# Linear attention and feed-forward on one core: w_phi loaded behind ScalarE's table load, and another order of steps behind the first key tile

## Chip, core, metric

The kernel runs on one core of a Trainium2 chip. The metric is the device time of one execution in microseconds (us). Before the change three runs took 228.24, 227.59 and 227.71 us, so the median is 227.71 us.

## What is computed

A block of a network over S = 2048 tokens of width D = 640 with H = 32 heads of 20 columns. `A` is linear attention with a learned feature map, `B` is a feed-forward layer of width 1728:

```python
qkv   = layernorm(x) @ wqkv                      # q, k, v: 32 heads x 20
pq,pk = q @ w_phi[h], k @ w_phi[h]               # per head, 20 x 20
phi   = concat(softmax(p), softmax(-p))          # 40 features of a head
kv, z = phi_k.T @ v, sum(phi_k)                  # over all 2048 tokens
o     = (phi_q @ kv) / (phi_q . z + 1e-6)
h     = x + o @ wo
out   = h + silu(layernorm(h) @ w1) @ w2
```

All tensors are bfloat16.

## The kernel before

The 2048 tokens are 16 tiles of 128 rows. The whole program is one list of named steps, ORDER; a step emits its instructions, and each engine and each DMA queue executes its own in the order of that list. Engines run beside each other and wait only for data and for buffers. So ORDER is six queues at once: TensorE, VectorE, ScalarE, GpSimd, SyncE with its DMAs, and ScalarE's own DMA queue, which only w_phi uses.

**Start.** Weights come in with X. `phi_a` and `phi_b` (VectorE, L305 and L308) make block-diagonal copies of w_phi's columns from the tile WPH, which is loaded by L183. `wk`, `fk` on TensorE transpose the key weights and fold phi into them (Wfk); `fq` (L437) does the same for queries, from the tile WTq, which the six steps `wq` (L425) load through a transposing DMA from DRAM.

**Keys, tile t.** `st` moments (VectorE), `rs` and `xn` normalise the row, `xt` transposes it into XnT: by TensorE for tiles 0 to 3, by a transposing DMA on SyncE's queue (L552) from tile 4 on. `K` and `V` (TensorE, L571, ten matmuls each) project, `ex` (ScalarE, L626) exponentials, `su` sums (VectorE, L630), `rk` inverse (ScalarE, L638 and L639), `sc` scale (VectorE, L643), `ve` copies the values (ScalarE), `kv` accumulates (TensorE, L662, eleven matmuls). `load0` to `load10` are the loads of wo, w1 and w2 (L563), which nothing needs before the later stages; they lie in SyncE's queue among the `xt`.

**Queries and attention.** `Q` (L609), `qe`, `qs`, `ql`, `qi`, `qr`, then `qt`, a transposing DMA into EqT. `bd` (VectorE) makes KVB from the accumulated kv. `D` (L817) applies it, `E` (VectorE, L826 and L827) divides, `ot` transposes O by a DMA (L839), `G` (L849, two steps of five matmuls for a tile) multiplies by wo, `ga` adds the residual (L856), `lm`, `ls`, `lr`, `hn`, `ht` are the second layernorm and its transpose.

**Feed-forward.** `u` (L931) and `s` (Silu) by units of two or four tiles. The product with w2 goes by pairs of tiles as seven products of half blocks in place of eight (`p1` to `p7`, L1036), with sums of weights (`T`, L1001) and of rows (`S`, L1018) ahead of them on VectorE, and `r`, `w` behind. `p7` needs S3 and T3; `p1` and `p2` need no sums. `out` stores.

**PSUM.** The key stage rotates three pairs of banks (`ps_pair`); a K, V, Q or fq step takes the pair whose last user lies three steps back, and waits until ScalarE or VectorE has read it. Later eight banks go round a ring.

Of the kernel before, what the change touches and what calls it, by code (L numbers as in the profile page):

```python
# [27 lines left out]
rk5 V8 ve8 V9 load4 rk7 sc5 st12 fq5 ve9 st14 rk6 xn11 rs12 K8 fq5e xt10 ref9 rs13 xn12 ex8 sc6 kv5 sc7
K9 su8 ref10 load1 V10 ex9 ve10 load5 kv6 eqr0 rs14 su9 Q0 K10 rk8 xn13 kv7 Q1 xt12 qe0 ref11 xt11 sc8
rk9 ref12 st15 sc9 xt13 xn14 kv8 rs15 K12 kv9 ex10 V12 su10 qe1 ex12 load0 K11 qs1 ve12 K13 xt14 rk10  # L30
su12 ex11 load10 qs0 ref13 V11 sc10 kv10 xn15 ex13 xt15 K14 su11 ql1 ve11 eqr1 rk12 V13 su13 qi1 ref15
# [10 lines left out]
D9 u2.0 u2.4 s2.12 u2.11 qs11 s2.0 ot8 s2.3 ls6 G81 G80 u2.7 qr10 qr11 E9 s2.11 u2.6 lr6 s2.6 qs14 s2.4
qt10 ga8 qs12 u2.5 qr12 lm8 u2.8 D10 out0 ot9 E10 qt11 s2.5 u2.10 hn6 ls8 G90 s2.7 u2.1 s2.8 s2.10 u2.9
out1 G91 qr14 u2.2 qs13 qr13 qt12 ga9 ot10 D11 s2.1 lt2 E11 ht6 s2.9 s2.2 S3.2 lm9 qt13 S1.2 ot11 lr8
hn8 ls9 p2.2 ht8 p1.2 lr7 D12 r1.2 S2.2 qt14 G101 G100 p7.2 p6.2 E12 r7.2 p4.2 lr9 hn7 ht7 G110 S4.2 hn9
ga10 S3.4 r2.2 w11.2 w21.2 G111 ot12 ga11 p7.4 p5.2 w22.2 lm10 r3.2 ht9 ls10 D13 lm11 ls11 p3.2 S1.4
p1.4 G121 S2.4 lr11 u6.1 r7.4 G120 r1.4 p6.4 w12.2 E13 p4.4 s6.1 ot13 ga12 D14 r2.4 w21.4 out3 E14 lm12
p5.4 ls12 lr12 u6.L w22.4 G131 r3.4 ot14 hn11 qs15 u6.3 G130 s6.L u6.2 qr15 u6.0 u6.9 ht11 s6.2 lr10
ga13 s6.0 p2.4 lm13 s6.9 w11.4 out5 hn12 u6.7 s6.3 hn10 G140 G141 u6.11 out2 s6.7 qt15 ht12 ls13 D15
S4.4 lr13 ht10 u6.12 u6.4 u6.10 s6.11 E15 ga14 hn13 s6.4 ht13 p3.4 w12.4 u6.5 u10.L ot15 s6.10 u6.8 s6.5  # L50
u6.6 s10.L lm14 s6.12 G151 s6.6 G150 lt6 S3.6 s6.8 S1.6 u10.2 ls14 p1.6 S2.6 r1.6 ga15 lm15 p7.6 r7.6
p6.6 u10.3 s10.2 p2.6 p4.6 S4.6 u10.6 s10.3 r2.6 p5.6 u10.8 u10.11 u10.9 lr14 s10.8 w21.6 S3.8 w22.6
r3.6 w11.6 p3.6 p7.8 hn14 p1.8 S1.8 s10.6 S2.8 ht14 u10.7 r1.8 p2.8 ls15 s10.9 p6.8 s10.11 s10.7 w11.8
lt10 w12.6 r7.8 u10.0 out4 u10.1 p4.8 r2.8 p5.8 lr15 u10.4 u10.10 r3.8 hn15 s10.0 w21.8 w22.8 u10.12
ht15 s10.4 s10.10 s10.12 u10.5 s10.1 u14.2 S4.8 s10.5 s14.2 S3.10 u14.12 u14.0 p2.10 out7 p7.10 S3.12
S1.10 s14.0 p3.8 p1.10 r7.10 S2.10 S4.10 out6 u14.10 p4.10 w12.8 s14.12 u14.L r1.10 u14.4 p6.10 s14.10
w11.10 p1.12 r2.10 p5.10 w21.10 u14.6 p7.12 w22.10 S1.12 s14.4 p2.12 s14.L r3.10 r7.12 r1.12 p3.10 S2.12
out8 s14.6 p4.12 w11.12 S3.14 p6.12 w12.10 out9 u14.8 s14.8 lt14 r2.12 w21.12 out11 p5.12 w22.12 p1.14
r3.12 S4.12 p7.14 S1.14 p3.12 out10 r7.14 S2.14 r1.14 p4.14 p6.14 out13 p2.14 S4.14 r2.14 w12.12 w11.14
w21.14 p5.14 p3.14 w22.14 out12 out140 r3.14 w12.14 out15 p3.14x out141 w12.14x out142  # L60
""".split()


# [1 line left out]
def kernel(  # L65
# [117 lines left out]
    nc.scalar.dma_start(WPH[:], A_w_phi.rearrange("h d f -> (h d) f").rearrange("(r p) f -> p r f", p=P))  # L183
# [15 lines left out]
    nc.scalar.preload_act_table_set("natural_log_exp_and_others")
# [935 lines left out]
```

## Time and profile before

| what | value |
|---|---|
| times of three runs, us | 228.24, 227.59, 227.71 |
| profiled execution, us | 227.59, of which the span is 225.7 |
| busy in the span | TensorE 218.2, VectorE 173.9, ScalarE 146.1, GpSimd 70.0 us |
| HBM read, written | 9.55, 2.62 MB |

A page of the profile lists busy time, the chain of work that ended last, the groups of instructions, and the DMAs. The other views are the waits (who waited for whom), the timeline (instructions in order of time, neighbours of one kind merged), and the answers for one line or one tile. `PE` is TensorE's matmul, `PEld` its weight load, `DVE` VectorE, `ACT` ScalarE, `POOL` GpSimd, `SPq` and `ACTq` the DMA queues of SyncE and ScalarE. In a timeline the columns are start, duration, engine, line, operation, output and input, count, and in brackets the idle time before it with what ended it.

### The profile page before, as it was taken

The numbers are of one execution on the slowest core, as the hardware profiler recorded it, in microseconds if no ns is written. First come the engines' busy times: TensorE is split into PE (matmuls) and PEld (weight loads), VectorE is DVE, ScalarE is ACT, GpSimd is POOL, SyncE is SP. The second block draws the span as 40 slices with busy tenths as digits, with TensorE's granted clock in tenths as the row PEclk, the third lists the DMA queues.
The fourth block names the chain that finished last, engine by engine and source line by source line (L and its number), as shares of the span: only waits on it lengthen the run. The fifth ranks groups of instructions, "written<-read, shape, count | busy, mean of one in ns | idle before, by whom it ended". The sixth has DMA issues, their size and how long they took to land.

```text
span 225.7 us, 5046 instructions
## 1 busy us (share of the span) xinstructions
PE 218.2 (97%) x1927; PEld 154.4 (68%) x1937; DVE 173.9 (77%) x305; ACT 146.1 (65%) x321; POOL 70.0 (31%) x136
## 2 busy tenths in 40 slices
...
GB/s 170 292 345 162 202 98 116 183 120 198 292 94 182 128 96 143 174 102 92 148 73 144 143 154 123 61 117 109 75 23 0 11 75 87 0 23 79 32 29 87
DMA packets 68158, 26.98 MB, mean 120 GB/s; under 512 B 61159, under 2 KB 67111, under 8 KB 68007
## 3 DMA queue, kind: packets, MB, share of 16 engines
...
q14 instruction: 8, 0.07, 0.1%
HBM read 9.55 MB, written 2.62 MB: 54 GB/s over the span
## 4 chain that ended last, share of the span: by engine, by line
PE 75%; DVE 14%; DMA 5%; issue 2%; ACT 2%; DVEq 0%; ACTq 0%
PE banks L931 25%; PE banks L1036 23%; PE banks L849 10%; PE banks L571 7%; PE banks L609 5%; DVE st L478 4%; DMA XnT<-xn 3%; PE banks L817 2%; DVE EK L643 2%; DVE Sk L630 2%; DMA OT<-O 2%; DVE Sq L737 1%; DVE xn L494 1%; PE banks L662 1%; ACT EK L626 1%
## 5 line engine op out<-in xcount | busy, mean ns | idle before, releaser
L931 PE MATMUL banks<-HnT,w_sb 128*128 128x512 bf16 (+1 forms) x315 | 59.8, 335 | 0.5
L954 ACT ACTIVATE shT<-banks 128x512 bf16<-128x512 f32 (+1 forms) x53 | 30.0, 587 | 45.2 <-PE banks L931 44.8
L931 PEld LDWEIGHTS <-w_sb 128*128 128x128 bf16 x325 | 31.2, 98 | 21.1
L571 PEld LDWEIGHTS <-XnT 128*128 128x128 bf16 x300 | 28.5, 98 | 10.9 <-DMA XnT<-xn 1.3
L494 POOL TENSOR_SCALAR xn<-X,mv,rs 128x640 bf16<-128x640 bf16 x12 | 30.8, 2565 | 1.5 <-ACT rs L485 1.3
L516 POOL TENSOR_SCALAR rs<-mv 128x1 f32<-128x1 f32 x16 | 4.7, 296 | 82.8 <-ACT xn L509 82.6
L1036 PEld LDWEIGHTS <-S 128*128 128x128 bf16 x231 | 22.1, 98 | 8.5
L1036 PE MATMUL banks<-T,S 128*128 128x320 bf16 x168 | 26.2, 299 | 0.0
L1051 DVE TENSOR_TENSOR o_t<-banks,r 128x320 bf16<-128x320 f32 (+2 forms) x33 | 15.1, 476 | 13.4 <-PE banks L1036 13.1
L849 PE MATMUL banks<-wo_sb,OT 128*128 128x320 bf16 x160 | 25.0, 299 | 0.4 <-DMA OT<-O 0.4
L1044 DVE TENSOR_TENSOR r<-banks,X 128x320 f32<-128x320 f32 x32 | 15.2, 485 | 12.9 <-PE banks L1036 12.8
L737 DVE TENSOR_REDUCE Sq<-EQ 128x66 f32<-128x1320 bf16 x16 | 24.3, 1519 | 0.0
L609 PE MATMUL banks<-Wfq,XnT 128*128 128x342 bf16 (+2 forms) x160 | 22.8, 293 | 0.0
L733 ACT ACTIVATE EQ<-banks 128x342 bf16<-128x342 f32 (+2 forms) x52 | 21.6, 527 | 1.9 <-PE banks L609 1.7
L571 PE MATMUL banks<-Wfk,XnT 128*128 128x304 bf16 x150 | 21.7, 292 | 1.0 <-DMA XnT<-xn 1.0
L571 PE MATMUL banks<-Wv,XnT 128*128 128x320 bf16 x150 | 22.5, 299 | 0.0
L630 DVE TENSOR_REDUCE Sk<-EK 128x64 f32<-128x1216 bf16 x16 | 21.9, 1402 | 0.4 <-ACT EK L626 0.4
L1036 PEld LDWEIGHTS <-shT 128*128 128x128 bf16 x168 | 16.3, 98 | 6.9
L626 ACT ACTIVATE EK<-banks 128x608 bf16<-128x608 f32 x32 | 20.3, 695 | 0.8 <-PE banks L571 0.8
L849 PEld LDWEIGHTS <-OT 128*128 128x128 bf16 x160 | 15.3, 98 | 7.4 <-DMA OT<-O 0.6
L609 PEld LDWEIGHTS <-XnT 128*128 128x128 bf16 x160 | 15.0, 97 | 5.4
L504 ACT ACTIVATE xn<-X 128x640 bf16<-128x640 bf16 x16 | 11.9, 745 | 10.0 <-DVE X L856 10.0
...
## 6 DMA issues: line engine op xcount, KB each, us to landing
...
```

The lines of the kernel that those rows point to most:

```text
L494: eng.tensor_scalar(out=xn_[t][:], in0=X[:, t, :], scalar1=mv_.pop(t)[:, 0:1], scalar2=rs_.pop(t)[:], op0=ALU.subtract, op1=ALU.mult,)
L571: nc.tensor.matmul(ps[:, g, 0:w], XnT[:, c, t * P : (t + 1) * P], W[:, c, g * w : (g + 1) * w], start=(c == 0), stop=(c == C - 1),)
L609: nc.tensor.matmul(ps[:, 0 : e - a], XnT[:, c, t * P : (t + 1) * P], Wfq[:, c, a:e], start=(c == 0), stop=(c == C - 1),)
L626: nc.scalar.activation(E5[:, :, :, b, 0:DR], p4, AF.Exp, scale=sign)
L630: nc.vector.tensor_reduce(sk[t][:], ek[t][:, 0 : H * HF].rearrange("p (q f) -> p q f", f=DH)[:, :, 0:DR], axis=AX.X, op=ALU.add)
L733: nc.scalar.activation(features(t, a, b)[:, :, :, i, 0:DR], p4, AF.Exp, scale=sign)
L737: nc.vector.tensor_reduce(sq[t][:], EQ[0][:, t, :, 0:FCH].rearrange("p c (q f) -> p c q f", f=DH), axis=AX.X, op=ALU.add)
L849: nc.tensor.matmul(ps_of["G", t][:, g, 0:HD], ot[t][:, c, :], wo_sb[:, c, g * HD : (g + 1) * HD], start=(c == 0), stop=(c == C - 1),)
L931: nc.tensor.matmul(ps[:, at : at + n], w1_sb[:, c, fc * P : fc * P + P], HnT[u][:, c, 0:n], start=(c == 0), stop=(c == C - 1),)
L954: nc.scalar.activation(rows_of(u)[:, f0 * n : f1 * n], ps_of.pop(("u", u, f0))[:, 0 : (f1 - f0) * n], AF.Silu)
L1036: nc.tensor.matmul(ps[:, lo:hi], left[:, c, :], right[:, c, lo:hi], start=(c == 0 and k in FIRST), stop=(c == KS - 1 and k in LAST), skip_ ...
L1044: nc.vector.tensor_tensor(r_[t, name][:], ps_of[bank, t][:, 0:HD], X[:, t + i, g * HD : (g + 1) * HD], op=ALU.add)
```

## The change

Two edits. The DMA that loads w_phi into WPH is emitted after the load of ScalarE's function table, where it was emitted before it; both lie on ScalarE's queue. And ORDER differs from its 105th step on, behind `xt3`: the same 899 steps with another sequence, on every engine and on SyncE's queue. No instruction is added or removed, no step changes its engine or its size.

```diff
-    nc.scalar.dma_start(WPH[:], A_w_phi.rearrange(...))
     w1_v = B_w1.rearrange("(c p) n -> p c n", p=P)
 ...
     nc.scalar.preload_act_table_set("natural_log_exp_and_others")
+    nc.scalar.dma_start(WPH[:], A_w_phi.rearrange(...))
```

The first lines of ORDER that differ, and those that hold the first attention tiles and the first products:

```diff
-wph0 K0.4 rs3 rs2 st4 K0.3 K1 V0.2 xn2 xt2 st5 ex0 rs4 ex1 V0.1 wph1 x2 V1 X8 ve1 xn3 wq3 xt3 V0.4 x3
-wq2 xn4 wq0 rs5 ve0 xn5 su0 rk0 V2 su1 st6 st7 rs6 sc0 K2 V3 xn6 rk1 ve2 xt4 ones5 rs7 K3 sc1 st11 kv0
-ex2 st8 kv1 ve3 ex3 load7 phq xt5 ones2 K4 rs8 load6 su3 ex4 rk3 xt6 su2 wq1 sc3 V4 st9 ve4 fq3 fq3e rk2
-xn7 V5 ref5 ve5 sc2 fq0 fq0e st13 rs9 K5 ref6 ex5 xn8 K6 fq2 kv2 ref7 ex6 xt7 su4 fq2e xn9 kv3 wq5 V6
-ve6 fq1 st10 fq1e K7 V7 zeros rs10 su5 xt8 rk4 sc4 fq4 xt9 ex7 ve7 rs11 kv4 fq4e ref8 ones6 xn10 su6 su7
 ...
+wph0 K0.4 rs3 rs2 st4 K0.3 K1 V0.2 xn2 xt2 st5 ex0 rs4 ex1 V0.1 wph1 x2 V1 X8 ve1 xn3 xt3 su0 st6 rk0
+xn4 V0.4 su1 x3 load10 ones5 wq0 sc0 K2 st7 rs5 st9 ve0 V2 xn5 rs6 xt4 xn6 ex2 rk1 sc1 ve2 ones2 rs9
+st12 wq3 xt5 phq V3 kv0 rs7 ve3 xt6 K3 K4 xn7 V4 ref5 kv1 ex3 ex4 st8 rs8 su2 su3 ve4 fq0 fq0e V5 fq3
+ref6 st10 rk2 xn8 ve5 wq2 K5 xn9 rk3 xt7 fq3e sc2 ex5 K6 ex6 kv2 wq1 sc3 su4 kv3 ref7 V6 su5 fq2 rk4 ve6
+K7 V7 rs12 fq2e ref8 su6 xn12 sc4 kv4 fq1 rs10 ex7 ve7 xt8 st15 rk6 ones6 xt9 fq1e zeros V8 st11 su7 fq4
+xn10 st14 ref9 ve8 rs11 wq5 sc6 rk5 fq4e xt12 xt10 rk7 V9 load7 sc5 ve9 K8 xn11 K9 sc7 fq5 kv5 fq5e kv6
 ...
-Q5 halves qt0 bd1 D0 qr2 D1 qe5 qs3 load9 Q4 qt2 E0 qe4 ql3 Q10 qe10 D2 E1 qs5 qi3 qr3 Q6 qe6 ot0 ot1
-G00 G01 ql5 qs4 E2 Q9 ql4 ga0 qi5 G11 qe9 qt3 G10 qr5 Q11 lm0 qi4 ls0 D3 qr4 ot2 lr0 qs6 ga1 Q8 qe11 lm1
+load5 qi2 halves qr2 qe7 D0 D1 qs3 ql3 E0 load6 Q4 qe4 Q10 qi3 qt2 E1 qr3 qs5 qe10 qs4 ql5 Q6 qe6 ot0 D2
+ot1 Q9 qe9 qi5 ql4 qr5 E2 G00 G01 ga0 lm0 ls0 qi4 G11 G10 qt3 Q11 qs6 qr4 D3 ga1 qe11 qt5 E3 lm1 lr0 hn0
 ...
-T2.0 lt0 u0.0 s0.6 G41 qr9 qt8 ot6 s0.12 G40 D8 s0.0 hn2 ot7 T2.1 p2.0 G61 T3.1 lr5 hn5 ga4 S1.0 p1.0
-S3.0 ls3 S2.0 p7.0 G60 lr3 lm4 E8 ht5 r1.0 ls4 G71 S4.0 lr4 w11.0 p6.0 ga6 hn3 T4.1 p3.0 r2.0 hn4 r7.0
+u0.12 ot6 s0.2 T2.2 D8 lr5 s0.8 T3.1 T3.0 lt0 ls3 S3.0 s0.10 ga4 hn5 E8 s0.12 ot7 T2.0 p7.0 S1.0 G61
+p1.0 T4.1 S2.0 p2.0 r1.0 r7.0 G60 ht2 p6.0 T4.0 T4.2 lr3 p4.0 G71 S4.0 r2.0 p3.0 lm4 p5.0 qr9 ls4 lr4
```

More of the change, by code (lines that the diff above doesn't have):

```diff
@@ L27 @@
-ve6 fq1 st10 fq1e K7 V7 zeros rs10 su5 xt8 rk4 sc4 fq4 xt9 ex7 ve7 rs11 kv4 fq4e ref8 ones6 xn10 su6 su7
[L28 to L31, printed above, removed]
@@ L32 @@
-eqp rk11 sc11 ql0 ref14 K15 qr1 rk13 load8 mask1 sc12 ex14 ve13 sc13 ex15 kv11 load2 Q2 V15 V14 qe2 su14
-qi0 su15 rk14 qr0 rk15 load3 ve14 Q3 qt1 ve15 sc14 kv12 kv13 sc15 kv14 qe3 kv15 Q7 qs2 ql2 qe7 qi2 bd0
-Q5 halves qt0 bd1 D0 qr2 D1 qe5 qs3 load9 Q4 qt2 E0 qe4 ql3 Q10 qe10 D2 E1 qs5 qi3 qr3 Q6 qe6 ot0 ot1
-G00 G01 ql5 qs4 E2 Q9 ql4 ga0 qi5 G11 qe9 qt3 G10 qr5 Q11 lm0 qi4 ls0 D3 qr4 ot2 lr0 qs6 ga1 Q8 qe11 lm1
-G20 E3 qs7 qr6 G21 qt5 Q12 hn0 ls1 ot3 ga2 lr1 qt4 qe8 Q13 qr7 D5 G31 E5 G30 hn1 ht0 ht1 ga3 qe12 qs8
@@ L37 @@
-Q14 ot5 qe13 qt6 qe14 Q15 qe15 padL0 D4 T1.0 qr8 u0.L u0.8 padL1 T1.2 E4 G50 G51 qt7 T3.0 lm2 s0.L T1.1
-ga5 s0.8 lm3 u0.10 s0.10 ls2 lm5 D6 T2.2 u0.4 u0.2 ot4 E6 D7 qs9 u0.6 u0.12 T3.2 s0.2 s0.4 E7 ls5 lr2
-T2.0 lt0 u0.0 s0.6 G41 qr9 qt8 ot6 s0.12 G40 D8 s0.0 hn2 ot7 T2.1 p2.0 G61 T3.1 lr5 hn5 ga4 S1.0 p1.0
-S3.0 ls3 S2.0 p7.0 G60 lr3 lm4 E8 ht5 r1.0 ls4 G71 S4.0 lr4 w11.0 p6.0 ga6 hn3 T4.1 p3.0 r2.0 hn4 r7.0
-T4.0 G70 p5.0 T4.2 ht2 qs10 ht3 ga7 p4.0 lm7 r3.0 ht4 qt9 w21.0 lm6 w12.0 u2.L ls7 s2.L u2.3 u2.12 w22.0
@@ L42 @@
[L42 to L60, printed above, removed]
+wph0 K0.4 rs3 rs2 st4 K0.3 K1 V0.2 xn2 xt2 st5 ex0 rs4 ex1 V0.1 wph1 x2 V1 X8 ve1 xn3 xt3 su0 st6 rk0
@@ new lines @@
+load3 kv7 ex8 ex9 st13 rs14 rs13 eqr0 su8 Q0 qe0 su9 ref10 rk8 rk9 xn13 K10 ref12 xn14 ex10 xt11 V10 sc8
+ve10 ref11 load9 Q1 kv8 V12 rs15 xn15 xt13 K12 qs0 qe1 su10 sc9 kv9 rk10 ve12 ref13 K11 load1 ex12 K13
+ex11 sc10 qs1 su12 xt14 ql0 ex13 ql1 V11 su11 su13 eqr1 rk12 rk11 load4 qi0 ve11 kv10 K14 xt15 sc11 rk13
+V13 ref14 sc12 eqp qr0 qi1 ex14 ve13 qr1 sc13 ref15 K15 load0 Q2 ex15 load2 kv11 kv12 su14 kv13 su15 V15
+qe2 qt0 rk14 qt1 rk15 V14 sc14 ve14 sc15 mask1 load8 ve15 Q3 qs2 kv14 ql2 kv15 Q5 bd0 qe3 qe5 Q7 bd1
@@ new lines @@
+load5 qi2 halves qr2 qe7 D0 D1 qs3 ql3 E0 load6 Q4 qe4 Q10 qi3 qt2 E1 qr3 qs5 qe10 qs4 ql5 Q6 qe6 ot0 D2
+ot1 Q9 qe9 qi5 ql4 qr5 E2 G00 G01 ga0 lm0 ls0 qi4 G11 G10 qt3 Q11 qs6 qr4 D3 ga1 qe11 qt5 E3 lm1 lr0 hn0
+Q8 ls1 D5 ot2 qt4 Q13 qr6 G20 qs7 lr1 G21 qe8 hn1 Q14 qe13 E5 Q15 qe14 ot3 Q12 ga2 G31 G30 ht0 qe15 qe12
+padL0 qs8 ht1 D4 u0.L ot5 T1.2 T1.0 qr7 s0.L T1.1 u0.0 lm2 padL1 qt6 ga3 E4 qt7 u0.6 qs9 G50 s0.0 qr8
+lm3 G51 T2.1 s0.6 D6 u0.4 ls2 s0.4 ga5 E6 u0.8 D7 ot4 lr2 lm5 qt8 u0.10 T3.2 u0.2 E7 G41 G40 ls5 hn2
@@ new lines @@
+u0.12 ot6 s0.2 T2.2 D8 lr5 s0.8 T3.1 T3.0 lt0 ls3 S3.0 s0.10 ga4 hn5 E8 s0.12 ot7 T2.0 p7.0 S1.0 G61
+p1.0 T4.1 S2.0 p2.0 r1.0 r7.0 G60 ht2 p6.0 T4.0 T4.2 lr3 p4.0 G71 S4.0 r2.0 p3.0 lm4 p5.0 qr9 ls4 lr4
+G70 ga6 hn3 ht5 w21.0 qs11 hn4 w22.0 ga7 ht3 ht4 u2.L lm6 u2.9 s2.L u2.1 qt9 r3.0 u2.7 ot8 w11.0 lm7
+w12.0 lt2 qr11 u2.10 s2.9 qs10 G81 qt11 s2.1 qr10 qs12 D9 u2.3 s2.3 s2.7 qt10 G80 E9 u2.5 ls6 lr6 u2.4
+s2.10 u2.2 ga8 u2.6 D10 ls7 u2.0 ot9 qr12 qt12 qs13 u2.12 s2.4 E10 lm8 D11 hn6 s2.5 ls8 ot10 u2.8 s2.0
@@ new lines @@
+qs14 E11 s2.6 s2.12 lr7 lr8 u2.11 G90 qr13 s2.2 D12 hn7 hn8 S3.2 ht6 s2.8 G91 p7.2 G101 qr14 ga9 s2.11
+S1.2 p1.2 S2.2 E12 G100 r1.2 out0 p2.2 ga10 qt13 ot11 lm9 p6.2 qt14 S4.2 D13 r2.2 r7.2 G110 G111 w11.2
+ls9 out1 S3.4 p4.2 E13 p5.2 ot12 ga11 lr9 w21.2 ht7 hn9 ht9 ht8 w22.2 ot13 D14 p7.4 r3.2 E14 lm11 p3.2
+qs15 S1.4 p1.4 S2.4 ls11 G121 r1.4 lm10 u6.L ls10 G120 u6.8 lr10 p6.4 r7.4 p4.4 ga12 S4.4 r2.4 lm12 qr15
+G131 w12.2 ot14 w21.4 G130 ga13 qt15 s6.L hn10 ls12 ht10 p5.4 lr11 s6.8 u6.11 G140 lm13 hn11 s6.11 u6.4
@@ new lines @@
+s6.4 lr12 D15 G141 u6.2 hn12 ls13 out3 r3.4 w22.4 p2.4 u6.5 s6.5 s6.2 E15 ga14 lr13 hn13 u6.1 w11.4 ht12
+u6.0 u6.3 lt6 u6.10 u6.7 out2 s6.10 s6.7 s6.3 s6.1 p3.4 w12.4 ht11 ht13 u6.6 s6.0 u10.L ot15 u6.12 u10.2
+s6.12 u10.9 s10.L G151 G150 s6.6 u6.9 S3.6 s10.2 u10.11 s6.9 S1.6 ga15 S2.6 lm15 u10.0 p7.6 s10.9 p1.6
+u10.6 lt10 lm14 S3.8 r1.6 s10.0 r7.6 s10.11 u10.7 s10.6 s10.7 u10.12 p4.6 S4.6 p6.6 p2.6 s10.12 r2.6
+p5.6 r3.6 ls15 w11.6 w21.6 u10.5 p2.8 S1.8 ls14 u10.3 w22.6 out5 lr15 u10.1 s10.5 p7.8 lr14 p1.8 S2.8
@@ new lines @@
+s10.3 hn14 u10.4 hn15 s10.1 r1.8 s10.4 ht14 w11.8 S3.10 p3.6 p6.8 ht15 r7.8 S4.8 u10.8 p4.8 out4 u14.4
+r2.8 w21.8 w12.6 s14.4 u10.10 p5.8 s10.8 w22.8 p3.8 r3.8 out6 u14.2 out9 w12.8 s14.2 s10.10 S1.10 u14.12
+p7.10 u14.10 out7 u14.L s14.12 u14.0 u14.6 p1.10 out8 S3.12 s14.0 s14.L r7.10 lt14 u14.8 S2.10 r1.10
+s14.6 p6.10 p4.10 s14.10 r2.10 p5.10 w21.10 r3.10 S4.10 p2.10 p7.12 p2.12 w11.10 w22.10 S1.12 p1.12
+S2.12 r1.12 w11.12 p3.10 p6.12 r7.12 p4.12 S4.12 r2.12 S3.14 w21.12 s14.8 w12.10 p5.12 p1.14 out11 r3.12
@@ L61 @@
+p7.14 S1.14 p3.12 S2.14 p2.14 r1.14 p6.14 w22.12 r7.14 out10 S4.14 w12.12 p4.14 r2.14 p5.14 w21.14
+w11.14 out12 p3.14x w22.14 p3.14 r3.14 w12.14x out13 out140 out15 out142 w12.14 out141
 """.split()
```

2 lines of the change are left out of this document (1 added, 1 removed).

## The prediction

> **What bounds the kernel now.** I read the page, then TensorE's waits, then the timeline around each of them. The page's first part says that TensorE is the bound:
>
> ```profile
> PE 218.2 (97%) x1927; PEld 154.4 (68%) x1937; DVE 173.9 (77%) x305; ACT 146.1 (65%) x321; POOL 70.0 (31%) x136
> ```
>
> The change neither adds nor removes a matmul, so a new order can only take idle time from TensorE, or give it some. Where that idle time lies, the waits of TensorE tell (total us, times, longest):
>
> ```profile
> PE banks L571 <- DMA XnT<-xn: 1.0, 1, 1.0
> PE banks L321 <- DMA Wk<-in_A_wqkv_dram: 0.9, 1, 0.9
> PE banks L231 <- PEq L1119: 0.8, 1, 0.8
> PE banks L849 <- DMA OT<-O: 0.4, 1, 0.4
> ```
>
> The second and third belong to the start, ahead of the step where the two orders part. What is left for the new order is small: one wait for a row that a DMA transposes into XnT, and one for OT. This is the first, in TensorE's timeline:
>
> ```profile
> 26.55 0.41 PE L437 MATMUL banks<-phi_q,WTq 128*128 128x114 bf16 x5
> 26.80 1.45 PE L571 MATMUL banks<-Wfk,XnT 128*128 128x304 bf16 x10
> 29.26 1.47 PE L571 MATMUL banks<-Wfk,XnT 128*128 128x304 bf16 x10 [1.01 <-DMA XnT<-xn]
> 30.57 0.41 PE L437 MATMUL banks<-phi_q,WTq 128*128 128x114 bf16 x5
> ```
>
> The rows are fq0, K5, K6, fq2. From K6 to its follower are 1.31 us, from K5 to K6 2.46, so K6 starts 1.15 us late. It waits for xt6, and SyncE's queue shows why that is late (xt4, load7, xt5, load6, xt6):
>
> ```profile
> 18.48 1.23 SPq L552 DMA_TRANSPOSE XnT<-xn  x1
> 19.76 0.58 SPq L563 DMA_DIRECT2D w_sb<-in_B_w_dram  x1
> 21.16 1.21 SPq L552 DMA_TRANSPOSE XnT<-xn  x1
> 22.41 0.59 SPq L563 DMA_DIRECT2D w_sb<-in_B_w_dram  x1
> 23.10 1.21 SPq L552 DMA_TRANSPOSE XnT<-xn  x1
> ```
>
> The answer for L552 gives what the twelve of them take from issue to landing:
>
> ```profile
> DMA to landing us min/median/max: 2.6/2.8/6.1
> ```
>
> The longest, 6.1, is xt6: issued at 23.10 it landed at 29.2, just where K6 starts. load6 stood in the queue right ahead of it. The second wait, for OT, is that of G00 behind Q6 (rows: Q4 and Q10, D2, Q6, G00):
>
> ```profile
> 70.03 2.77 PE L609 MATMUL banks<-Wfq,XnT 128*128 128x342 bf16 x20
> 72.64 0.52 PE L817 MATMUL banks<-KVB,EqT 128*128 128x63 bf16 x12
> 73.00 1.47 PE L609 MATMUL banks<-Wfq,XnT 128*128 128x342 bf16 x10
> 74.83 1.40 PE L849 MATMUL banks<-wo_sb,OT 128*128 128x320 bf16 x9 [0.36 <-DMA OT<-O]
> ```
>
> Two Q steps take 2.61 us there, one 1.31; Q6 to G00 is 1.83, so 0.52 us are lost.
>
> **The change part by part.** *K6's wait.* In the new order load7 goes behind xt10 and load6 behind xt15, and xt6 follows xt5 directly, with wq3 ahead of xt5. On TensorE the same steps stand ahead of K6. xt5 ran at 21.16, so xt6 can be issued at 22.4; with the median of 2.8 us it lands at 25.2, and K6 is due at 26.80 + 1.31 = 28.1. Even 5.7 us would do. I take the whole wait: -1.15 us, bounds -1.15 and 0 (if xt6 is slow for another reason).
>
> *G00's wait.* Q9 moves ahead of G00, and D2 behind Q6. Q9's 1.31 us cover the 0.52 us: -0.52, bounds -0.52 and 0.
>
> *A new wait at fq3.* wq3 moves on SyncE's queue from ahead of xt4 to behind it, so it is issued at 19.7 at the earliest. fq3 takes the place of fq0 as the last of V4, fq, V5, fq, so it is due at 26.55. The answer for WTq gives the landing of the six wq:
>
> ```profile
> DMA to landing us min/median/max: 3.7/6.4/7.5
> ```
>
> That is 26.1 by the median and 27.2 by the worst: a wait of 0 to 0.65 us. I take 0.2, since the long ones were issued right behind X8, the largest load of X, and wq3 will no longer be. The other wq have more room: wq2 and wq1 lie behind xt6 and xt7, fq2 and fq1 behind K6.
>
> *VectorE must follow.* TensorE can use 1.67 us only where VectorE is ahead too. VectorE's own large gap in the key stage hangs on the same late row, through K6, ex6 and rk4:
>
> ```profile
> 34.90 0.83 DVE L643 TENSOR_TENSOR EK<-EK,Rk 128x1280 bf16<-128x1280 bf16 x1 [1.56 <-ACT Rk L639]
> ```
>
> Following K6, ex6, rk4 and sc4 by hand in the new order with the durations of these rows I find VectorE ahead by 1.3 us from sc4 on, an estimate. It gets tightest at the first product of the feed-forward. p7.0 becomes the first one and loses p2.0, G61 and p1.0 ahead of it; S3.0, which it needs, loses T2.0, qr9, ga4 and S1.0 ahead of it. VectorE's rows are T2.0, T2.1, ga4, and S1.0 with S3.0; TensorE's are p2.0 and p7.0:
>
> ```profile
> 99.41 0.48 DVE L1001 TENSOR_TENSOR T<-w_sb,T 128x640 bf16<-128x640 bf16 x1
> ...
> 100.88 0.48 DVE L1001 TENSOR_TENSOR T<-w_sb,T 128x640 bf16<-128x640 bf16 x1
> ...
> 101.68 0.82 DVE L856 TENSOR_TENSOR X<-banks,X 128x640 bf16<-128x640 f32 x1
> 102.42 1.15 DVE L1018 TENSOR_TENSOR S<-shT 128x896 bf16<-128x896 bf16 x2
> ```
>
> ```profile
> 101.66 1.11 PE L1036 MATMUL banks<-w_sb,shT 128*128 128x320 bf16 x7
> ...
> 104.23 1.11 PE L1036 MATMUL banks<-T,S 128*128 128x320 bf16 x7
> ```
>
> S3.0 ends at 102.42 + 1.15 = 103.57; less T2.0 and qr9 (1.47), ga4 (0.74) and S1.0 (about half of 1.15) that is 100.8. p7.0 moves to 101.66. With both engines moved alike there are 0.86 us to spare; with TensorE 1.67 ahead and VectorE 1.3, 0.5 us; with VectorE not ahead at all TensorE waits 0.8. I take +0.2, bounds 0 and 0.8.
>
> *w_phi.* ScalarE's timeline and the answers for WPH show what the load is worth:
>
> ```profile
> 0.78 0.46 ACTq L183 DMA_DIRECT2D WPH<-in_A_w_phi_dram  x1
> 1.27 1.28 ACT L199 ACT_TABLE_LOAD   x1 [1.27 <-PEq L1119]
> 5.95 0.69 ACT L338 COPY WTk<-banks 128x640 bf16<-128x640 bf16 x1 [3.40 <-PE banks L321]
> 6.54 0.67 ACT L354 CAST Wfk<-banks 128x608 bf16<-128x608 f32 x1
> ```
>
> ```profile
> L305 DVE TENSOR_TENSOR WPD<-WPH x1: 205/205/205, 4.2 to 4.2; 128x95 bf16<-128x95 bf16 x1
> ...
> DMA to landing us min/median/max: 2.7/2.7/2.7
> ```
>
> It lands at 3.5 and is first read at 4.2, 0.7 us later; ScalarE itself is idle until 5.95, so a table that is ready 0.5 us earlier brings nothing. Does the DMA have to wait for the table? The CAST at 6.54 started while the COPY before it still ran to 6.64: the queue hands out the next instruction without waiting for the last one's end. So I take the DMA to go out at about 0.85 beside the table load: 0, and that is the lower bound. The upper bound: issued at 0.78 + 1.28 = 2.06, and landing as late as the two small loads of the same tensor on SyncE's queue, by the answer for WPQ:
>
> ```profile
> DMA to landing us min/median/max: 4.8/5.3/5.7
> ```
>
> That is 6.9 to 7.8 where 4.2 was wanted, up to +3.6 us; with its own 2.7 it is 4.8, +0.6.
>
> The second table load, ahead of the first Silu, shows that nothing follows the 1.28 us:
>
> ```profile
> 92.09 1.28 ACT L970 ACT_TABLE_LOAD   x1
> 93.38 0.28 ACT L970 ACTIVATE SHL<-banks 128x128 bf16<-128x128 f32 x1
> ```
>
> The Trainium skill, page "ScalarE: Activation LUTs", section "What ACT_TABLE_LOAD costs", puts a drain of about 1.38 us to the load's 1.28; the trace has the load and not the drain. By the page, if the DMA waited for both, w_phi would land at about 6.1 and the sum would come out some 1.9 us higher, as an estimate at 228.3.
>
> *The end.* The last two products swap: the piece of 128 columns goes ahead of that of 192, and their stores with them. Both are in the same queues on each engine as before, one behind the other: 0.
>
> *Sum.* -1.15 - 0.52 + 0.2 + 0.2 + 0 = -1.27 us. The profiled execution took 227.59 us, 225.7 of it the span: 226.3. The median of the runs is 0.12 above it: 226.4.
>
> **The rivals.** *The wait stays.* xt6 still lands late: now wq3 is ahead of it and wq2 behind, and a wq takes 6.4 us by the median where a bare xt takes 2.8; or a later row waits, since the loads that left this place go among xt11 to xt15. For it speaks that the DMAs carry the same bytes in the end; against it, that K6 has almost 3 us to spare. Then only G00's part remains, less the small waits: 227.71 - 0.52 + 0.2 = 227.4. Chance 0.2.
>
> *w_phi comes late (slower).* If ScalarE's queue holds the DMA until the table is loaded, WPD waits, and everything on VectorE behind it, in order: phi, xn0, the moments, the first sums. VectorE has no slack to make it up (its only large gap in the key stage is the 1.56 us above), and TensorE waits for Wfk and XnT. It decides from a landing at 4.2 + 1.27 = 5.5: later than that the kernel is slower than before. At 4.8 it is still 227.0, at 6.9 it is 226.4 + 2.7 = 229.1. For it speaks that the change puts the DMA there; against it, the overlapping rows. Chance 0.13.
>
> *VectorE becomes the bound.* It is not ahead, p7.0 waits 0.8 us, and the products behind it, whose sums of weights and rows move in the same way, some tenths more: about 227.3. Its waits are for ScalarE and TensorE, which speaks against it. Chance 0.1.
>
> **How the numbers follow.** The forecast has 0.57. Its own range is 225.8 (both waits gone and no new one, 227.71 - 1.67 = 226.0, less 0.2 for waits too short for the view) to 227.0. The range of 8 in 10 leaves out only the latest landings of w_phi and a wait that I have not seen: 225.8 to 228.8. About 0.3%, or 0.68 us, is what a measurement tells from no change, so faster is below 227.03 and slower above 228.39. Faster: nearly all of the forecast (0.55) and a quarter of the first and third rivals (0.07), together 0.62. Same: most of these two (0.18), the early half of w_phi (0.04), a rest of the forecast (0.01): 0.23. Slower: the late half of w_phi (0.09) and 0.06 for those of the other cases where a wait in the feed-forward is added: 0.15.
>
> **What the profile after would show.** Right: TensorE's waits no longer list XnT, or only tenths; load6 and load7 far behind xt6, and xt6 landing in about 3 us; G00 without OT's wait; WPD at 4.2; the gap ahead of sc4 under 0.5 us; p7.0 at about 100. Wrong: a wait of TensorE for WTq or for XnT at K10 to K15; WPD later than 4.5, with DMA WPH as what ended VectorE's idle time; S or T as the releaser of L1036.

## Result and the profile after

Four runs of the changed kernel took 226.05 to 226.19 us, median 226.17; the kernel before took 227.65 (median of four). The ratio is 0.993, with a 95% interval of 0.9911 to 0.9948: 1.5 us faster, where the prediction said 1.3 (226.4). The profiled execution took 226.15 us with a span of 224.4, against 227.59 and 225.7. Here and below, executions over 1.5% slower than the fastest of their kernel are left out of ratios and intervals, and no trace of one is read.

The page's line of busy time and TensorE's waits, after:

```profile
PE 218.7 (97%) x1937; PEld 154.5 (69%) x1937; DVE 173.8 (77%) x305; ACT 144.7 (64%) x321; POOL 72.5 (32%) x136
```

```profile
PE banks L231 <- PEq L1119: 0.8, 1, 0.8
PE banks L321 <- DMA Wk<-in_A_wqkv_dram: 0.8, 1, 0.8
PE banks L345 <- ACT rs L484: 0.3, 1, 0.3
PE banks L530 <- DVE xn L494: 0.2, 1, 0.2
PE banks L662 <- DVE EK L643: 0.2, 1, 0.2
```

The waits for XnT and OT are gone. The first four are of the start; the last is new: a kv step (kv3) waits for a scale of VectorE (sc3). SyncE's queue, after (xt4, wq3, xt5 with xt6, wq2):

```profile
17.62 1.23 SPq L552 DMA_TRANSPOSE XnT<-xn  x1
18.90 1.27 SPq L425 DMA_TRANSPOSE WTq<-in_A_wqkv_dram  x1
21.41 2.54 SPq L552 DMA_TRANSPOSE XnT<-xn  x2
24.00 1.26 SPq L425 DMA_TRANSPOSE WTq<-in_A_wqkv_dram  x1
```

From issue to landing the answers for L552 and for L425 give:

```profile
DMA to landing us min/median/max: 2.6/2.6/3.8
```

```profile
DMA to landing us min/median/max: 2.9/3.9/7.2
```

xt6 goes out at 22.73 and takes 2.6: it is down at 25.3, where it was 29.2 before. TensorE there (fq3; K5 with K6; kv2; kv3; V6):

```profile
26.41 0.41 PE L437 MATMUL banks<-phi_q,WTq 128*128 128x114 bf16 x5
26.66 2.75 PE L571 MATMUL banks<-Wfk,XnT 128*128 128x304 bf16 x20
29.25 0.50 PE L662 MATMUL banks<-VP,EK 128*128 128x63 bf16 x11
29.94 0.51 PE L662 MATMUL banks<-VP,EK 128*128 128x63 bf16 x11 [0.19 <-DVE EK L643]
30.29 1.52 PE L571 MATMUL banks<-Wv,XnT 128*128 128x320 bf16 x10
```

K5 and K6 are one row now, with nothing between them. But kv3 starts 0.69 behind kv2 where V6 follows kv3 after 0.35: it starts only when VectorE's scale is done. kv4 is late as well. These rows are V7, kv4 and, further down, V9, after:

```profile
33.19 1.52 PE L571 MATMUL banks<-Wv,XnT 128*128 128x320 bf16 x10
34.67 0.51 PE L662 MATMUL banks<-VP,EK 128*128 128x63 bf16 x11
...
36.88 1.52 PE L571 MATMUL banks<-Wv,XnT 128*128 128x320 bf16 x10
```

From V7 to its follower are 1.48 us, where before (V7, fq4) they are 1.36:

```profile
34.39 1.52 PE L571 MATMUL banks<-Wv,XnT 128*128 128x320 bf16 x10
35.75 0.41 PE L437 MATMUL banks<-phi_q,WTq 128*128 128x114 bf16 x5
```

For the stretch from 29 to 36 the answer for L662 gives what ended the idle time ahead of kv3 and kv4 (TensorE's and its weight loads' added up):

```profile
  DVE EK L643: 0.8, 3
```

Q6 to G00 (rows: Q4, Q10 and Q6; D2; Q9; G00), without a wait:

```profile
69.26 4.08 PE L609 MATMUL banks<-Wfq,XnT 128*128 128x342 bf16 x30
73.17 0.52 PE L817 MATMUL banks<-KVB,EqT 128*128 128x63 bf16 x12
73.53 1.47 PE L609 MATMUL banks<-Wfq,XnT 128*128 128x342 bf16 x10
74.84 1.38 PE L849 MATMUL banks<-wo_sb,OT 128*128 128x320 bf16 x9
```

And the start of ScalarE with its DMA, and WPD on VectorE:

```profile
0.78 1.28 ACT L198 ACT_TABLE_LOAD   x1 [0.78 <-PEq L1119]
0.81 0.46 ACTq L199 DMA_DIRECT2D WPH<-in_A_w_phi_dram  x1
...
4.13 0.20 DVE L305 TENSOR_TENSOR WPD<-WPH 128x95 bf16<-128x95 bf16 x1
```

The DMA goes out 0.03 us behind the start of the table load, 1.25 ahead of its end, and w_phi is in time.

Matching the first matmul of each step in the two traces gives the account. Only steps that have the same steps ahead of them in both orders can be compared. K5 is 0.14 us earlier than before and K6 1.30 (27.96 for 29.26), so 1.16 came at K6. V9 is 0.82 earlier: 0.48 was lost on the way, nearly all of it at kv3 (0.35) and kv4 (0.12). The last key step kv15 is 0.77 earlier, so behind V9 hardly anything was lost. D3, the first such D step behind G00, is 1.31 earlier, and so are the last products, so 0.54 came at G00. That is the whole 1.3 us of the span: 0.14 + 1.16 - 0.53 + 0.54 = 1.31.

### The profile page after: what moved, and what is told of

It reads as the page before. It is cut to its first block, busy times and chain, and to the rows that moved or that the text cites. A ratio compares the mean times of both kernels' runs of the same rounds, so it can differ in the third digit from the quotient of the medians.

```text
span 224.4 us, 5053 instructions
## 1 busy us (share of the span) xinstructions
PE 218.7 (97%) x1937; PEld 154.5 (69%) x1937; DVE 173.8 (77%) x305; ACT 144.7 (64%) x321; POOL 72.5 (32%) x136
## 4 chain that ended last, share of the span: by engine, by line
PE 85%; DVE 8%; DMA 4%; SPq 1%; issue 0%; DVEq 0%
PE banks L931 25%; PE banks L1036 23%; PE banks L571 11%; PE banks L849 10%; PE banks L609 9%; DVE st L478 3%; DMA X<-in_A_x_dram 3%; PE banks L817 3%; DVE Sk L630 2%; PE banks L662 2%; DMA Wk<-in_A_wqkv_dram 2%; DVE EK L643 1%; PE banks L942 1%; DVE mv L479 1%; DVE xn L494 1%; PE banks L437 0%
## 5 line engine op out<-in xcount | busy, mean ns | idle before, releaser
L931 PE MATMUL banks<-HnT,w_sb 128*128 128x512 bf16 (+1 forms) x325 | 60.7, 336 | 0.0
L954 ACT ACTIVATE shT<-banks 128x512 bf16<-128x512 f32 (+1 forms) x53 | 29.5, 587 | 32.1 <-PE banks L931 32.0
L494 POOL TENSOR_SCALAR xn<-X,mv,rs 128x640 bf16<-128x640 bf16 x12 | 32.4, 2700 | 1.6 <-ACT rs L485 1.3
L516 POOL TENSOR_SCALAR rs<-mv 128x1 f32<-128x1 f32 x16 | 3.5, 219 | 80.2 <-ACT xn L509 79.9
L1036 PE MATMUL banks<-T,S 128*128 128x320 bf16 x168 | 26.7, 299 | 0.0
L849 PE MATMUL banks<-wo_sb,OT 128*128 128x320 bf16 x160 | 25.3, 299 | 0.0
L571 PE MATMUL banks<-Wfk,XnT 128*128 128x304 bf16 x150 | 21.2, 292 | 0.0
```

What stands on the lines that cost most here:

```text
L494: eng.tensor_scalar(out=xn_[t][:], in0=X[:, t, :], scalar1=mv_.pop(t)[:, 0:1], scalar2=rs_.pop(t)[:], op0=ALU.subtract, op1=ALU.mult,)
L571: nc.tensor.matmul(ps[:, g, 0:w], XnT[:, c, t * P : (t + 1) * P], W[:, c, g * w : (g + 1) * w], start=(c == 0), stop=(c == C - 1),)
L849: nc.tensor.matmul(ps_of["G", t][:, g, 0:HD], ot[t][:, c, :], wo_sb[:, c, g * HD : (g + 1) * HD], start=(c == 0), stop=(c == C - 1),)
L931: nc.tensor.matmul(ps[:, at : at + n], w1_sb[:, c, fc * P : fc * P + P], HnT[u][:, c, 0:n], start=(c == 0), stop=(c == C - 1),)
L954: nc.scalar.activation(rows_of(u)[:, f0 * n : f1 * n], ps_of.pop(("u", u, f0))[:, 0 : (f1 - f0) * n], AF.Silu)
L1036: nc.tensor.matmul(ps[:, lo:hi], left[:, c, :], right[:, c, lo:hi], start=(c == 0 and k in FIRST), stop=(c == KS - 1 and k in LAST), skip_ ...
```

## Experiments

All times are ratios to runs of the kernel before on the same chip, with 95% intervals. In these series the kernel before spread by several us from run to run, so an interval reaches about 0.4 us or more to either side.

| run | ratio | interval | us: (ratio - 1) x 227.65 |
|---|---|---|---|
| after | 0.9930 | 0.9911 to 0.9948 | -1.6 |
| e1: w_phi alone | 1.0015 | 0.9989 to 1.0041 | +0.3 |
| e2: order alone | 0.9939 | 0.9915 to 0.9964 | -1.4 |
| e3: two loads back | 0.9945 | 0.9928 to 0.9962 | -1.3 |
| e4: Q9 alone | 0.9985 | 0.9964 to 1.0007 | -0.3 |
| e5: e3 and e4 | 0.9951 | 0.9931 to 0.9971 | -1.1 |
| e6: after, loads returned | 1.0006 | 0.9978 to 1.0035 | +0.1 |
| e7: after, w_phi late | 1.0153 | 1.0122 to 1.0184 | +3.5 |
| e8: after, kv3 and kv4 later | 0.9945 | 0.9924 to 0.9967 | -1.3 |
| e9: after, xt6 behind wq2 | 0.9960 | 0.9939 to 0.9980 | -0.9 |
| e10: e5 and qt8 | 0.9939 | 0.9912 to 0.9966 | -1.4 |
| e11: e8 and eqr0 | 0.9940 | 0.9920 to 0.9960 | -1.4 |
| e12: one exchange | 0.9922 | 0.9895 to 0.9949 | -1.8 |

**e1, e2: the two edits apart.** e1 is the kernel before with the DMA's line moved, e2 the kernel after with the line moved back:

```diff
 e1
-    nc.scalar.dma_start(WPH[:], ...)
 ...
     nc.scalar.preload_act_table_set("natural_log_exp_and_others")
+    nc.scalar.dma_start(WPH[:], ...)
```

> The kernel before with the move of w_phi alone; ORDER as before. Theory (the DMA goes out beside the table load): its issue at about 0.81, WPD at 4.1 to 4.2, time equal to the kernel before within 0.15 us. Rival (w_phi is late, and the new order had more to give than was measured): issue after 2.06, WPD later than 4.5, time 0.6 us or more above the kernel before.

> The kernel after with w_phi's DMA back ahead of the table load, so the new ORDER alone. Theory (the order makes the whole gain): 226.2, as the kernel after within 0.15 us, 1.4 to 1.5 below the kernel before. Rival (the move of w_phi brings part of the gain, by the 0.07 us that the start was earlier or more): 226.3 to 226.7.

Both theories held: moving w_phi alone changes nothing that can be measured (the interval is -0.3 to +0.9 us; the DMA went out at 0.8, and WPD came at 4.4, a little behind the expected 4.2, without a wait), and the order alone makes the gain (median 226.20). In e1's profiled execution, whose order and queue are those of before, the wait for XnT is

```profile
PE banks L571 <- DMA XnT<-xn: 0.3, 1, 0.3
```

where before had 1.0: xt6 took 5.4 us in place of 6.1. The wait that the change removes is not a fixed price.

**e3: only the two loads.**

```diff
-ex2 st8 kv1 ve3 ex3 load7 phq xt5 ones2 K4 rs8 load6 su3 ex4 rk3 xt6
+ex2 st8 kv1 ve3 ex3 phq xt5 ones2 K4 rs8 su3 ex4 rk3 xt6
 ...
-K15 qr1 rk13 load8 mask1 sc12 ex14 ve13 sc13 ex15 kv11 load2 Q2
+K15 qr1 rk13 load8 load7 mask1 sc12 ex14 ve13 sc13 ex15 kv11 load2 load6 Q2
```

> The kernel before with only load7 and load6 moved back on SyncE's queue, behind xt15; every other engine's list is unchanged. Theory (xt6 was late because load6 stood right ahead of it): xt6 issued at about 21.9, landing about 24.7, K6 without a wait at about 28.1; time 0.8 to 1.15 below the kernel before, since the gain at K6 may fade to 0.77 at the end of the keys as it did after the change. Rival A (xt6 was late because of the wq loads or of code that DMAs fetched at 26.3): xt6 still takes 5 to 6 us to land and K6 waits 0.3 to 1 us; time 0 to 0.4 below. Rival B (another row, xt11 to xt15, waits in its place): XnT as releaser at K11 to K15, time 0.2 to 0.6 below.

The theory held. xt4, xt5 and xt6 stand in one row of SyncE's queue, each lands in 2.6 us, and the wait that is left is OT's:

```profile
18.39 5.29 SPq L552 DMA_TRANSPOSE XnT<-xn  x3
```

```profile
PE banks L849 <- DMA OT<-O: 0.5, 1, 0.5
```

K6 is 1.19 earlier than before, and kv15 still 1.19: unlike in the new order nothing is lost in the key stage. OT's wait grows by 0.14, and the span is 1.0 shorter.

**e6: the loads put back into the changed kernel.**

```diff
-st12 wq3 xt5 phq V3 kv0 rs7 ve3 xt6
+st12 wq3 load7 xt5 phq V3 kv0 rs7 ve3 load6 xt6
 ...
-rk7 V9 load7 sc5
+rk7 V9 sc5
 ...
-ql3 E0 load6 Q4
+ql3 E0 Q4
```

> The kernel after with load7 put back ahead of xt5 and load6 ahead of xt6 on SyncE's queue; all else as after. Theory (a bulk load ahead in the queue makes the transposing DMA late): xt5 takes 3.4 to 4.2 us to land and xt6 5.4 to 6.8 instead of 2.6, K6 waits 0.3 to 1.2 us for XnT, time 0.3 to 1.2 above the kernel after, and wider scattered than its runs. Rival (the wq rows around them, which the new order also moved, made the difference): xt6 lands in 2.6 to 3.5, no wait, time as after.

The theory held, and the loss is larger than it said: the whole gain is gone (ratio 1.0006, so about 1.7 us above the kernel after). With e3, the loads' place is enough to give the gain and to take it. Only the times of this kernel are used here.

**e9: no load near, but xt6 later.**

```diff
-st12 wq3 xt5 phq V3 kv0 rs7 ve3 xt6
+st12 wq3 xt5 phq V3 kv0 rs7 ve3 wq2 xt6
 ...
-ve5 wq2 K5
+ve5 K5
```

> The kernel after with wq2 moved on SyncE's queue from behind xt6 to ahead of it; nothing else. No bulk load is near; xt6 goes out at about 24.0 instead of 22.7, and the trace of after shows a fetch of program code by a DMA of the instruction queue (16 KB, queue 8) at 25.1, in the middle of its flight. Theory (two things made xt6 late before: the bulk load pushed it back, and there it met this fetch, which holds up what is in flight): xt6 takes 3.9 to 6 us and lands at 27.9 to 30, K6 waits 0.1 to 2 us for XnT, time 0.1 to 1.2 above the kernel after. Rival (the bulk loads alone made it late): xt6 takes 2.6 to 3.0, lands at 26.6 to 27.0, no wait, time as after.

The theory held, in its lower half. xt6 went out at 24.53; a fetch of program code followed at 25.69; the answer for it and TensorE's wait:

```profile
DMA to landing us min/median/max: 4.8/4.8/4.8
```

```profile
PE banks L571 <- DMA XnT<-xn: 0.8, 1, 0.8
```

The time is 226.66, 0.5 above the kernel after (the two intervals overlap at their ends). So a late xt6 needs no bulk load. What the late ones share is a fetch of 16 KB by the DMA queue that the page calls "q8 instruction": by the packets of the traces it came at 26.30 before, 26.18 in e1, 24.79 in e3 and 25.07 after. In the first two xt6 was still in flight then, held back by load6; in the last two it had landed, or nearly.

e9 by itself can't tell the fetch from wq2, which now stands directly ahead of xt6. e7 (below) can: its queue has the order of the kernel after, with xt5 directly ahead of xt6. There xt6 went out at 28.74, a fetch came at 30.80, and xt6 took 4.5 us where it took 2.6 in the kernel after:

```profile
DMA to landing us min/median/max: 4.5/4.5/4.5
```

The other transposing DMAs agree, in the thirteen traces without e6's. Those into HnT, the transpose behind the second layernorm, took 2.55 to 2.70 us when no such fetch fell into their flight (148 of them), and 3.05 to 4.73 when one came between 0.5 and 2.2 us after their issue (21 of them). The traces show one thing more: on SyncE's queue no DMA landed ahead of one that was issued before it. So an xt behind a slow transfer is late with it.

What DMAs do around such a fetch, before, in windows (length, TensorE busy, clock, DMA share, GB/s), with xt6 in flight until 29.2:

```profile
26.00:27.00 1.00, 1.00 (x13) 1.00 2.18 233
27.00:28.00 1.00, 1.00 (x10) 1.00 0.28 15
```

For a whole microsecond next to nothing moves. (The page has a second queue of program code, q14; it has 8 KB in flight from 26.46 to 28.19 here, but nothing in the hole that e5 shows below.) wq2 in the kernel after, out at 24.00 and so 1.1 ahead of a fetch, took 4.8 us; wq3 and wq1, with no q8 fetch near, took 3.0 and 3.1. A wq directly ahead costs an xt something too: xt8, right behind wq1, takes 3.6 with no q8 fetch near. Of the 2.2 us that xt6 loses in e9 the fetch therefore has some 1.2, an estimate from xt8's 3.6; the loss to the wq alone would still have been no wait (24.53 + 3.6 = 28.1, where K6 could start at about 28.4, 1.3 behind K5's 27.11).

The Trainium skill, page "Runtime: NRT & Kernel Launch", section "Instruction fetch mechanics", says that a program is refilled in blocks of 16 KiB over a DMA queue of the sequencer and that the cost is "mostly hidden". The blocks are here (15 on q8), and TensorE stays busy through both windows; but a transposing DMA that is in flight pays.

**e12: the smallest edit.**

```diff
-K4 rs8 load6 su3 ex4 rk3 xt6 su2 wq1
+K4 rs8 su3 ex4 rk3 xt6 load6 su2 wq1
```

> The kernel before with one exchange on SyncE's queue: xt6 ahead of load6 in place of behind it. load7 stays ahead of xt5, and load6 now stands between xt6 and wq1, xt7. Theory (xt6 was late by load6 ahead of it and by the code fetch at about 26.3 that it then met): xt6 goes out at about 22.4, takes 2.6 to 3.6 us, is down by 26, before the fetch, and K6 starts at about 28.0 without a wait; time 0.9 to 1.4 below the kernel before, as with both loads moved far back. Rival (load7 counts too, or load6 now holds up xt7 and fq1): xt6 4 us or more, or a wait for xt7 at K7 or for WTq at fq1; time 0 to 0.7 below.

The theory held. Rows: load7; xt5 and xt6; load6; wq1.

```profile
19.55 0.58 SPq L563 DMA_DIRECT2D w_sb<-in_B_w_dram  x1
21.26 2.54 SPq L552 DMA_TRANSPOSE XnT<-xn  x2
23.86 0.57 SPq L563 DMA_DIRECT2D w_sb<-in_B_w_dram  x1
24.49 2.21 SPq L425 DMA_TRANSPOSE WTq<-in_A_wqkv_dram  x1
```

xt6 goes out at 22.57 and lands in 2.6 at 25.2, the fetch comes only at 24.9, K6 is 1.08 earlier than before and the last product 1.25. One exchange of two DMAs in one queue is worth as much as the whole new order (median 226.03, ratio 0.9922; the intervals overlap, so no more can be said).

**e4, e5, e10: what Q9 ahead of G00 is worth.** e4 moves Q9 in the kernel before, e5 does this and e3's edit, e10 adds qt8 ahead of lt0:

```diff
-Q6 qe6 ot0 ot1 G00 G01 ql5 qs4 E2 Q9
+Q6 qe6 ot0 ot1 Q9 G00 G01 ql5 qs4 E2
 ... (e10)
-T2.0 lt0 u0.0 s0.6 G41 qr9 qt8 ot6
+T2.0 qt8 lt0 u0.0 s0.6 G41 qr9 ot6
```

> The kernel before with only TensorE's step Q9 moved from behind E2 to ahead of G00. Theory (Q9's 1.31 us cover the wait for OT, and TensorE is the bound from there on): no wait for OT at G00, time 0.4 to 0.5 below the kernel before. Rival (the wait is given back: Q9 now waits for its pair of banks, or Q11 and D3 behind it come to wait for ScalarE, or VectorE is the bound in the feed-forward): time 0 to 0.2 below.

> The kernel before with both single edits: load7 and load6 moved back behind xt15, and Q9 moved ahead of G00. Theory (the two waits are the whole change, and the new order loses about 0.4 us elsewhere that these two edits don't lose): no wait for XnT or OT, span 224.1 to 224.3, time 225.6 to 225.9, which is 0.3 to 0.5 us below the kernel after. Rival (OT's wait is given back later, as the 0.15 us of the single edit of Q9 may be read): 226.1 to 226.4, as with the loads alone.

> The kernel before with load7 and load6 behind xt15, Q9 ahead of G00, and qt8 ahead of lt0 on SyncE's queue. With the first two edits alone D8 waited 0.8 us for qt8, which went out at 94.05, 1.3 us ahead of a code fetch at 95.3, and took 6.1 us. Theory (the gain at G00 was lost there alone): qt8 goes out at about 92.8, takes 3 to 4 us, D8 without a wait at 99.4, p7.0 at about 102.2; time 225.5 to 225.8, 0.6 to 0.8 below the same kernel without the last edit and below the kernel after. Rival (VectorE, or lt0 which now meets the fetch, is late next): a wait for S, T or shT at L1036, time 226.1 to 226.4.

Theory fell in e4 and e5. e4's time decides nothing (its interval is -0.8 to +0.2 us), but its trace gains 0.54 us from kv15 to D3 and has lost 0.37 of it at D8. In e5 OT's wait does go as well: against e3, e5 is 0.32 earlier at K6 and 1.02 earlier at D3. But at D8 all but 0.04 of that is gone:

```profile
PE banks L817 <- DMA EqT<-EQ: 0.8, 1, 0.8
```

D8 needs qt8. It went out at 94.05, a fetch came at 95.30, and the windows of e5 show the same hole as above, with 0 GB/s; it lands at 100.2, after 6.1 us:

```profile
95.00:96.00 1.00, 1.00 (x20) 1.00 3.59 145
96.00:97.00 1.00, 1.00 (x11) 1.00 0.00 0
97.00:98.00 1.00, 1.00 (x11) 1.00 0.07 8
```

In e10 qt8 goes out at 93.17, takes 4.9 and is in time: D8 doesn't wait, and between u0.L and p7.0 e10 gains 0.93 on e5 in the traces. Since e10's execution began 0.41 later (K6), 0.52 of it is left at the end; the median is 226.20 against 226.36, and the intervals overlap, so by time this step is inconclusive. In the kernel after qt8 goes out at 93.66, ahead of lt0, and takes 3.1; the fetch comes at 96.14, 2.5 us into its flight. That the new order keeps the gain at G00 because it moved this DMA as well is argued from e5 and e10; no run moves it back.

**e8, e11: where the 0.53 us in the key stage went.**

```diff
 e8, against after
-kv2 wq1 sc3 su4 kv3 ref7 V6
+kv2 wq1 sc3 su4 ref7 V6 kv3
 ...
-sc4 kv4 fq1 rs10 ex7 ve7 xt8 st15 rk6 ones6 xt9 fq1e zeros V8
+sc4 fq1 rs10 ex7 ve7 xt8 st15 rk6 ones6 xt9 fq1e zeros V8 kv4
 ... (e11 also)
-V9 load7 sc5 ve9 K8 xn11 K9 ... rs14 rs13 eqr0
+V9 load7 sc5 ve9 K8 K9 ... rs14 rs13 eqr0 xn11
```

> The kernel after with TensorE's kv3 moved from ahead of V6 to behind it, and kv4 from ahead of fq1 to behind V8. Theory (of the 1.43 us that K6 comes earlier about 0.4 go lost because kv3 and kv4 now stand at VectorE's heels and wait for sc3 and sc4): no wait of L662 for EK, V9 and later steps 0.3 to 0.5 earlier, time 225.7 to 225.9. Rival (VectorE is the bound there, so the next step that needs it, kv5 or a K step for its EK buffer, waits the same): time as after, 226.1 to 226.2.

> The kernel after with kv3 behind V6, kv4 behind V8 (as before), and on GpSimd xn11 behind eqr0 in place of ahead of it. With the two kv alone 0.2 us were gained by V9 and gone by K12: V12 waited for its banks behind rk8 and ex10 on ScalarE, which stood behind qe0, which waited for eqr0; eqr0 stood behind xn11, which took 4.24 us on GpSimd beside three scale steps of VectorE where the others take 2.5. Theory (that chain is what gives the gain back): eqr0 at about 42, qe0 about 0.8 earlier, V12 and K12 0.2 to 0.4 earlier than in the kernel after, time 225.7 to 225.95. Rival (yet another wait takes its place, such as XnT for K11 or K13, or kv9 for sc9): time as after, 226.1 to 226.25.

In e8 the idle time ahead of kv3 and kv4 is gone, and V9 is 0.20 earlier measured from K6 (V8 starts 0.28 late there, which it doesn't in e11); by K11 it is all given back. The chain behind that: three scales of VectorE run back to back (first row, of after), beside them xn11 takes 4.24 us on GpSimd where the median of its twelve is 2.5, eqr0 comes behind it, and ScalarE waits (third row, of e8), late then with rk8 and ex10.

```profile
38.89 2.25 DVE L643 TENSOR_TENSOR EK<-EK,Rk 128x1280 bf16<-128x1280 bf16 x3
...
39.10 4.24 POOL L494 TENSOR_SCALAR xn<-X,mv,rs 128x640 bf16<-128x640 bf16 x1
```

```profile
44.01 0.70 ACT L733 ACTIVATE EQ<-banks 128x627 bf16<-128x627 f32 x1 [0.89 <-POOL EQ L460]
```

The Trainium skill, page "SBUF — State Buffer", section "SBUF: two separate sides", lets only one of VectorE and GpSimd have a shared pair of ports, for a whole instruction, when VectorE reads two SBUF operands as a scale does. The trace agrees in one direction: xn11, begun beside the first scale, loses 1.74 us and ends 2.2 us behind the last scale. It does not in the other: sc4 (33.78, 0.83 us) runs inside an xn of 2.50 us that began at 33.06, and neither is slower than elsewhere. In e11 eqr0 doesn't stand behind xn11 any more, and xn11 comes after the scales:

```profile
40.74 0.58 POOL L460 MEMSET EQ<- 128x264 f32 x1 [1.76 <-PE banks L437]
41.20 2.51 POOL L494 TENSOR_SCALAR xn<-X,mv,rs 128x640 bf16<-128x640 bf16 x1
```

From K6 to V9 e11 takes 8.43 us, exactly as e3 does in the old order, where the kernel after takes 8.92: so kv3 and kv4 are all that the key stage lost up to V9. Against the kernel after V9 is 0.42 earlier, qe0 0.80, K12 0.43, kv15 0.28, the last product 0.29: what e8 gave back between V9 and K11 isn't given back here. The profiled execution took 225.82, but the median of its runs is 226.22, with the kernel after's in its interval. The chain is shown by the traces; that e11 is the faster kernel isn't.

**e7: the price of a late w_phi.**

```diff
     nc.scalar.preload_act_table_set("natural_log_exp_and_others")
+    nc.scalar.preload_act_table_set("silu_and_others")
+    nc.scalar.preload_act_table_set("natural_log_exp_and_others")
     nc.scalar.dma_start(WPH[:], ...)
```

> The kernel after with two more loads of a function table on ScalarE ahead of w_phi's DMA (this table, another one, this one again), so that w_phi comes late on purpose; ScalarE has nothing else to do until 5.9. Theory (the queue hands the DMA out while the last table load runs, as in the kernel after, but only then): the DMA goes out at about 3.4, lands at about 6.0, WPD at 6.0, and by the prediction's arithmetic (landing less 4.2) the time is 1.8 above the kernel after, 228.0. Rival A (the start has slack: the rows and Wfk wait for other things): 0.3 to 1.0 above. Rival B (the DMA does not wait for the engine's work at all): issue at 0.8, nothing lost.

```profile
0.79 2.57 ACT L198 ACT_TABLE_LOAD   x2 [0.79 <-PEq L1119]
3.05 0.46 ACTq L199 DMA_DIRECT2D WPH<-in_A_w_phi_dram  x1
3.36 1.28 ACT L198 ACT_TABLE_LOAD   x1
...
9.37 0.26 DVE L305 TENSOR_TENSOR WPD<-WPH 128x95 bf16<-128x95 bf16 x1 [5.19 <-DMA WPH<-in_A_w_phi_dram]
...
10.84 0.91 PE L345 MATMUL banks<-phi,WTk 128*128 128x228 bf16 x6 [5.62 <-DVE WTk L338]
```

The DMA goes out at 3.05, while the second table load still runs and ahead of the third: the queue runs ahead of ScalarE's work. But from there, among the loads of X and the weights, w_phi takes 6.3 us and not 2.6. WPD is 5.2 us later than in the kernel after, and the median, 230.92, is 4.75 above it. Nearly every microsecond of lateness is paid, as the prediction's rival had it; the landing was mis-sized in the expectation by 3.4 (9.4 for 6.0).

## Why the prediction was right, point by point

- **K6's wait** (-1.15). Issue at 22.73 for 22.4, landing at 25.3 for 25.2, no wait: right, and 1.16 came at K6. Another 0.14 was there at K5 already; in the runs that keep TensorE's order of before up to there, K5 lies between 0.59 later and 0.34 earlier, so this is scatter. What the prediction did not see is why xt6 was late: it named load6 directly ahead and left everything else to "another reason". The other part is the code fetch that xt6 then met (e9, e7). load6 was down at 26.38, just as the fetch began; xt5 landed 1.1 behind load7, and the same pass would have had xt6 down at 27.5, ahead of K6's 28.1. By this estimate load6 without the fetch would have cost nothing; e1's 0.3 and before's 1.0 show how loose the price is.
- **G00's wait** (-0.52). 0.54 in the two traces: right in size. Here too the prediction didn't ask why the transfer was late; a fetch stands there as well (behind this list). That the gain lasts was taken for granted; e4 and e5 show that it doesn't by itself. The step left out was D8 behind it, whose qt8 the new order moved too.
- **A new wait at fq3** (+0.2). Wrong, harmlessly: 0. wq3 went out at 18.90, before the "earliest" of 19.7, since xt4 had gone at 17.62 and not 18.48, and it took 3.0 us, less than the fastest wq before (3.7).
- **VectorE must follow** (+0.2, bounds 0 to 0.8). The size was within its bounds, the place was wrong. At p7.0 nothing was lost: p7.0 starts at 100.35 for "about 100", and S3.0, the row `98.92 0.62`, was done 0.8 us before. VectorE's sc4 came at 33.78 for 34.90, 1.1 us ahead where 1.3 was estimated. It wasn't enough in the key stage: 0.53 us went there, 0.47 of it at kv3 and kv4 behind sc3 and sc4, and next to nothing behind V9. eqr0's chain is the next limit, met only when these two are moved (e8). The third rival named this cause, with another place and a larger price.
- **w_phi** (0). Right: 0.81 for 0.85, WPD at 4.13, and e1 shows no effect beyond its interval. The argument from two overlapping rows of ScalarE carried to a DMA of its queue. e7 bears out the rival's price.
- **The end** (0). Right: the last product is 1.31 earlier, the span 1.3.
- **The sum.** -1.27 forecast; -0.14 - 1.16 + 0.53 - 0.54 = -1.31 in the traces. The two waits were sized right. The VectorE term was 0.33 too small, fq3's 0.2 too large, and 0.14 came by scatter; these nearly cancel, so that the sum is this close is luck. The first rival, that the wait stays, fell as its counter-argument said: K6 had 2.5 us to spare (25.3 to its first weight load at 27.83).

OT's transfer, ot0, went out at 71.21 in the kernel before, a fetch of program code came at 71.90, and the answer for ot0 is

```profile
DMA to landing us min/median/max: 3.6/3.6/3.6
```

In the thirteen traces the 140 transposes into OT with no such fetch in their flight took 2.55 to 3.24 us, their median 2.6. With 2.6 OT would have been down at 73.8, and G00 was due at 74.3. So, by these estimates, neither of the two waits that the change took away would have been there without a fetch.

Open: why DMAs stand still for about a microsecond behind a code fetch; whether load6 without a fetch would have made K6 wait at all (the estimate above says no, no run shows it); and whether e11 or e12 beats the changed kernel.
